# The second mixture of experts with its first product by Strassen's algorithm, in 3 passes of 768 tokens

## The chip, the cores and the metric

The kernel runs on one core of one Trainium2 chip. The metric is device time in microseconds (us) of one execution, as the median of several runs. The core has five engines that take their instructions in order and wait for each other by semaphores: TensorE (PE in the profile, with its weight loads as PEld), VectorE (DVE), ScalarE (ACT), GpSimd (POOL) and SyncE (SP), which issues nearly all DMAs here.

## The reference

Three parts follow each other on 2304 tokens of 512 features: a linear attention, a first mixture of experts with one expert per token, and the part that is changed, a second mixture in which every token goes through all 8 experts.

```
def _moe2_ref(x, w_gate, w1, w2):          # x 2304 x 512, 8 experts, hidden size 1024
    logits = x @ w_gate
    P = np.exp(logits - logits.max())
    for _ in range(8):                     # Sinkhorn steps
        P /= P.sum(1, keepdims=True) + 1e-09
        P /= P.sum(0, keepdims=True) + 1e-09
        P *= N / E
    for e in range(E):
        h = np.maximum(x @ w1[e], 0.0)     # first product
        out += P[:, e:e + 1] * (h @ w2[e]) # second product
```

All tensors are float32.

## The kernel before

Precision. TensorE multiplies in a one-pass float32 type (F32R in the code). To keep float32 accuracy each operand is split in two such parts, a high part (a copy by ScalarE into F32R) and a low part (the difference, by VectorE or GpSimd), and each product is three products: high by high, high by low, low by high. So the names come in pairs: `w1h`, `w1l`, `x2h`, `x2l`, `hh`, `hl`, `w2h`, `w2l`.

The second mixture is `moe2`. It is a generator: its first part, up to `yield`, is written after the attention and prepares the weights `w1` of expert 0 while the first mixture (`moe1`) runs; the rest starts when the rows of `x2d`, the result of the first mixture in device memory, are complete. All 18 tiles of 128 tokens are loaded into `acc`, transposed on TensorE (L836) and split into `x2h` and `x2l`, which stay in SBUF for all experts. The tokens form 5 chunks, one of 256 tokens and four of 512.

For each expert, chunk and block `f` of 128 hidden features, `first` (L895) makes 12 matmuls into one PSUM tile `ph` (4 blocks of the 512 features, 3 products each), ScalarE takes the relu into `hh` (L898) and VectorE the low part `hl` (L899). `second` (L908) multiplies the block of the step before with `w2`, 3 matmuls of 512 columns for each tile of tokens, into up to 4 PSUM tiles `py` that gather over the 8 blocks; VectorE adds each finished `py`, times its gate, to `acc` (L918). So on TensorE a first product and a second product of the block before always alternate, and the relu of one block has the time of the other product to be done in.

The weights of the next expert are loaded and split (`load_w`, L784 to L791) while the last chunk of an expert runs, through three buffers `rw` of 256 KB. Router logits come from 8 matmuls per chunk during expert 0 (L847), the Sinkhorn steps (L872 to L886) follow in the last chunk of expert 0; a step has a chain of small VectorE operations with one small matmul `pc` (L881) in it.

Each engine's order is the one that a scheduler gives to the instructions as they are written. Pools give out SBUF and PSUM tiles under a tag with a number of buffers, and an instruction that writes a reused buffer waits for the last reader of its former content.

Of the kernel before, what the change touches and what calls it, by code (L numbers as in the profile page):

```python
# [7 lines left out]
F32 = mybir.dt.float32  # L8
# [10 lines left out]
P = 128  # L19
# [13 lines left out]
CHUNKS = ((0, 2), (2, 4), (6, 4), (10, 4), (14, 4))  # first tile of P tokens, tiles  # L33
NCH = len(CHUNKS)
CH = 4 * P
NH = 3
# [6 lines left out]
def attention(tc, nc, cp, q, k, v, w_phi, w_gate, w_skip, lgs, routed, stepped, keys_done, last_steps):  # L43
    """routed(bp, x, hp, lg): rows of x for one head pair are complete; lg after the last one.
    stepped(): after each step. keys_done(): after each step once the keys' tiles are released.
    last_steps(psum): before the last products"""
    with ExitStack() as ctx:
# [15 lines left out]
        # per head: [I | w_gate | w_skip], so that one product yields num, den and logits  # L63
# [88 lines left out]
        def prep_v(u):  # L152
            # v = vh + vl, with a column of ones for the denominator
# [124 lines left out]
        # work that keeps the tensor engine busy beside the steps: (unit offset, call) by step  # L278
# [39 lines left out]
        # step t: projections of t, exponentials of t - 1, transposes and products of t - 2  # L318
# [58 lines left out]
def constants(tc, nc, keep, pool):  # L377
# [4 lines left out]
    # strictly upper ones (prefix over partitions) and ones, exact in bfloat16  # L382
# [21 lines left out]
    # of each expert: the slots of more than half a slot's tokens, then (as if of 8 more) the others  # L404
# [4 lines left out]
    # tri[v, w] = 1 for w <= v  # L409
# [13 lines left out]
class Router:  # L423
    """gates and expert of each token; lists of tokens by expert; the table of slots"""
# [8 lines left out]
    def route(self, bp, lg):  # L433
# [6 lines left out]
        # gate = 1 / (sum exp(l - max) + 1e-9) for tokens that compute  # L440
# [9 lines left out]
        # first index of the maximum  # L450
# [9 lines left out]
        # rank of a token among those of its expert, and the counts  # L460
# [26 lines left out]
        # the places of two tokens differ, so the scatters need no order among themselves  # L487
# [18 lines left out]
    def scatter(self, n=NJ):  # L506
        """n more of the scatters of the batches routed last"""
        for _ in range(min(n, len(self.todo))):
            self.todo.pop(0)()

    def early_slots(self):
        """slots 0 and 1: each the next tokens of the expert with the most left of batches 0 and 1"""
# [4 lines left out]
        for i in range(2):  # L517
# [24 lines left out]
            # tokens that the early slots take, by expert  # L542
# [9 lines left out]
    def slots(self):  # L552
        """of the slots after those: numbers of full and of all, each one's expert and first place"""
# [16 lines left out]
        # first place of slot s: bs[v(s)] + SLOT * s  # L570
# [28 lines left out]
def moe1(tc, nc, c, rt, w1, w2, idx, xd, xd0, x2d, route):  # L599
    """generator: slot 0's loads; then slot 0 and the others"""  # L600
# [171 lines left out]
def moe2(tc, nc, c, w_gate, w1, w2, x2d, out):  # L772
    """generator: the first weights; then the rest"""
    with ExitStack() as ctx:
        sm = ctx.enter_context(tc.tile_pool(name="m2s", bufs=2, reuse_waits="tile"))
        wp = ctx.enter_context(tc.tile_pool(name="m2w", bufs=1, reuse_waits="tile"))
        NKB, NFB = D // P, FF // P
        w1h, w1l = [wp.tile([P, NKB, FF], F32R, name=nm) for nm in ("w1h", "w1l")]

        def load_w(src, e, i):  # L780
            r = sm.tile([P, 512], F32, name="rw", tag="rw", bufs=3)
            if src is w1:
                kb, h = divmod(i, 2)
                nc.sync.dma_start(r, w1[e, kb * P : kb * P + P, 512 * h : 512 * h + 512])  # L784
                sl = slice(512 * h, 512 * h + 512)
                dh, dl = w1h[:, kb, sl], w1l[:, kb, sl]
            else:
                nc.sync.dma_start(r, w2[e, i * P : i * P + P])
                dh, dl = w2h[:, i], w2l[:, i]
            nc.scalar.activation(dh, r, AF.Copy)  # L790
            (nc.gpsimd if i % 3 == 1 else nc.vector).tensor_tensor(dl, r, f32(dh), ALU.subtract)  # L791

        for i in range(8):
            load_w(w1, 0, i)
# [248 lines left out]
```

## Time and profile before

| what | value |
|---|---|
| median of 3 runs | 2152.64 us (2148.99 to 2154.48) |
| the profiled execution, first to last instruction | 2155.2 us |
| TensorE busy | 2078.2 us, 96% |
| VectorE, ScalarE, GpSimd busy | 793.3, 592.0, 314.5 us |
| first matmul of a first product of the second mixture | at 548.48 us |
| groups on L895 and L908 (the second mixture's two products) | 3840 and 3456 matmuls |
| share of the last chain on TensorE | 81%, of it L895 36%, L908 36% |

A row of the timeline gives start, duration, engine, line, operation, tiles and the number of instructions merged. Matmuls are pipelined, so their durations overlap: the pace is read from start to start. A row of groups gives the count, then busy time and the mean of one in ns, then the idle time of the engine ahead of them. The granted clock is a share of 2.4 GHz.

### The profile page before, as it was taken

The page shows a single profiled execution, that of the slowest core. Times are in us where ns is not written, and L with a number is a line of the kernel's source. Part 1 is how long each engine was busy: PE and PEld are TensorE (multiplying, and loading weights), DVE is VectorE, ACT ScalarE, POOL GpSimd, SP SyncE. Part 2 cuts the span into 40 slices and gives each one's busy share as a digit, 9 for nine tenths or more (in the row PEclk, how much of TensorE's full clock was granted, in tenths as well). Part 3 has the DMA queues.
Part 4 walks back from the last instruction along what each step waited for, and adds up shares of the span by engine and source line. Part 5 has one row for each costly group of instructions (what it writes and reads, how often), then busy time and mean ns, then how long its engine had stood idle before and what let it go on. Part 6 is the DMA issues. An engine that isn't in the chain of part 4 may idle for free.

```text
span 2155.2 us, 26804 instructions
## 1 busy us (share of the span) xinstructions
PE 2078.2 (96%) x10809; PEld 1772.0 (82%) x10809; DVE 793.3 (37%) x1376; ACT 592.0 (27%) x1147; POOL 314.5 (15%) x248
## 2 busy tenths in 40 slices
PE   6999878998899999999999999999999999999999
PEld 6998867887788878888888888888888888888887
DVE  6888875786311341132123212211321232122112
ACT  4776554454321241121112112211211121122110
POOL 4445244565000000000001000000100010000000
PEclk9999898999899999999999999999999999999999
DMA  4587397564300110010002001100200020011001
GB/s 92 86 124 90 54 211 173 209 229 156 128 1 1 40 40 1 1 59 20 1 1 79 1 0 35 45 0 1 64 15 1 1 78 1 1 40 35 20 20 39
DMA packets 129992, 117.93 MB, mean 55 GB/s; under 512 B 70914, under 2 KB 94210, under 8 KB 129472
## 3 DMA queue, kind: packets, MB, share of 16 engines
q1 hardware_dynamic: 126400, 109.02, 20.4%
q0 software_dynamic: 3456, 7.09, 0.9%
q8 instruction: 87, 1.43, 0.3%
q14 instruction: 49, 0.40, 0.1%
HBM read 97.64 MB, written 20.81 MB: 55 GB/s over the span
## 4 chain that ended last, share of the span: by engine, by line
PE 81%; DMA 4%; DVE 2%; issue 1%; ACT 0%; POOL 0%; POOLq 0%; SPq 0%; DVEq 0%; ACTq 0%
PE ph L895 36%; PE py L908 36%; PE ph L687 3%; PE py L721 2%; DMA xg<-xd,ix 2%; DMA rw<-in_moe_w_dram 1%; DMA xd<-x 1%; PE pn L237 1%; DVE w2l L652 0%; PE pt L836 0%; PE pg L847 0%; PE ptq L221 0%; PE pt L664 0%; DMA x2d<-yo,ix 0%; POOL w1l L652 0%
## 5 line engine op out<-in xcount | busy, mean ns | idle before, releaser
L899 DVE SCALAR_TENSOR_TENSOR hl<-ph,hh 128x512 fp32r<-128x512 f32 (+1 forms) x320 | 203.8, 637 | 1088.2 <-ACT hh L898 1088.2
L898 ACT ACTIVATE hh<-ph 128x512 fp32r<-128x512 f32 (+1 forms) x320 | 177.5, 555 | 1164.1 <-PE ph L895 1162.3
L908 PE MATMUL py<-w2h,hh 128*128 128x512 f32 x1152 | 449.9, 391 | 0.0
L908 PE MATMUL py<-w2h,hl 128*128 128x512 f32 x1152 | 449.2, 390 | 0.0
L908 PE MATMUL py<-w2l,hh 128*128 128x512 f32 x1152 | 448.7, 390 | 0.0
L895 PE MATMUL ph<-x2h,w1h 128*128 128x512 f32 (+1 forms) x1280 | 317.6, 369 | 0.7 <-ACT x2h L838 0.7
L895 PE MATMUL ph<-x2h,w1l 128*128 128x512 f32 (+1 forms) x1280 | 316.7, 369 | 0.0
L895 PE MATMUL ph<-x2l,w1h 128*128 128x512 f32 (+1 forms) x1280 | 316.0, 369 | 0.0
L895 PEld LDWEIGHTS ph<-x2h,w1h 128*128 128x128 f32 x1280 | 231.7, 189 | 45.8 <-ACT x2h L838 1.1
L895 PEld LDWEIGHTS ph<-x2l,w1h 128*128 128x128 f32 x1280 | 228.4, 189 | 39.9
L895 PEld LDWEIGHTS ph<-x2h,w1l 128*128 128x128 f32 x1280 | 228.1, 189 | 39.7
L908 PEld LDWEIGHTS py<-w2l,hh 128*128 128x128 f32 x1152 | 216.3, 188 | 45.4
L908 PEld LDWEIGHTS py<-w2h,hh 128*128 128x128 f32 x1152 | 216.5, 188 | 42.9
L908 PEld LDWEIGHTS py<-w2h,hl 128*128 128x128 f32 x1152 | 216.5, 188 | 42.4
L791 POOL TENSOR_TENSOR w2l<-rw,w2h 128x512 fp32r<-128x512 f32 x24 | 31.0, 1290 | 1262.6 <-ACT w2h L790 1262.6
L358 POOL TENSOR_TENSOR fl<-f,fh 128x1024 fp32r<-128x1024 f32 (+1 forms) x40 | 86.5, 2162 | 117.8 <-DVE fh L357 64.5
L918 DVE SCALAR_TENSOR_TENSOR acc<-py,lg,acc 128x512 f32<-128x512 f32 x126 | 85.9, 741 | 2.1 <-PE py L908 2.1
L790 ACT ACTIVATE w2h<-rw 128x512 fp32r<-128x512 f32 x64 | 40.2, 633 | 82.0 <-PE py L908 74.7
L652 DVE TENSOR_TENSOR w2l<-r,w2h 128x512 fp32r<-128x512 f32 x48 | 60.5, 1260 | 3.5
L790 ACT ACTIVATE w1h<-rw 128x512 fp32r<-128x512 f32 x64 | 39.0, 630 | 73.8 <-DMA rw<-in_moe_w_dram 63.7
L687 PE MATMUL ph<-xTh,w1h 128*128 128x256 f32 x288 | 48.5, 292 | 11.1 <-ACT xTh L666 7.0
L791 DVE TENSOR_TENSOR w1l<-rw,w1h 128x512 fp32r<-128x512 f32 x40 | 33.5, 849 | 68.5 <-ACT w1h L790 47.5
(228 smaller groups left out, 2308.2 us busy)
## 6 DMA issues: line engine op xcount, KB each, us to landing
r<-in_moe_w_dram SPq DMA_DIRECT2D x76, 512.0 KB, 5.8
rw<-in_moe_w_dram SPq DMA_DIRECT2D x128, 256.0 KB, 2.8
xd<-x SPq DMA_DIRECT2D x12, 576.0 KB, 15.4
qt<-in_q_dram SPq DMA_DIRECT2D x32, 144.0 KB, 3.6
x2d<-x SPq DMA_DIRECT2D x8, 576.0 KB, 3.8
out_dram<-acc SPq DMA_DIRECT2D x18, 256.0 KB, 2.1
kt<-in_k_dram SPq DMA_DIRECT2D x32, 128.0 KB, 2.7
vt<-in_v_dram SPq DMA_DIRECT2D x32, 128.0 KB, 3.0
```

Of the source, the lines that this page charges most:

```text
L237: nc.tensor.matmul(pn, w[:, b, h, fb], r[:, h, fb, b], start=(c == 0), stop=(c == 5))
L358: nc.gpsimd.tensor_tensor(fl[:, :n], f[:, :n], f32(fh)[:, :n], ALU.subtract)
L652: (nc.gpsimd if pool and i % 3 == 1 else nc.vector).tensor_tensor(dl, src, f32(dh), ALU.subtract)
L687: nc.tensor.matmul(ph, wt[:, kb, f * P : f * P + P], xt[:, kb], start=(n == 0), stop=(n == 11))
L721: nc.tensor.matmul(py, ht[:, f, a * P : a * P + P], wt[:, f], start=(n == 0), stop=(n == 23))
L790: nc.scalar.activation(dh, r, AF.Copy)
L791: (nc.gpsimd if i % 3 == 1 else nc.vector).tensor_tensor(dl, r, f32(dh), ALU.subtract)
L895: nc.tensor.matmul(ph, wt[:, kb, f * P : f * P + P], xt[:, kb], start=(m == 0), stop=(m == 11))
L898: nc.scalar.activation(hh, ph, AF.Relu)
L899: nc.vector.scalar_tensor_tensor(hl, ph, 0.0, f32(hh), ALU.max, ALU.subtract)
L908: nc.tensor.matmul(ys[i], ht[:, i * P : i * P + P], wt[:, f], start=(f == 0 and n == 0), stop=(f == NFB - 1 and n == 2),)
L918: nc.vector.scalar_tensor_tensor(acc[:, t], ys[i], lg[:, t, e : e + 1], acc[:, t], ALU.mult, ALU.add)
```

## The change

`moe2` is written anew; attention, first mixture and router are as before, but for removed comments and constants.

The tokens go in 3 passes of 768, each made of a half of 384 tokens from either half of the batch. Within a pass all experts run, each in 2 "quads" of 4 blocks of 128 hidden features, so there are 48 quads. A quad's first product is a 2 x 2 block product: features in 2 halves, hidden blocks in 2 x 2, tokens in 2 halves. Strassen's algorithm, in Winograd's form with shared sums, gives the four results from 7 block products of half the depth instead of 8, at the price of sums of blocks ahead of the products (of weights on GpSimd, `sums_w1`, of tokens on VectorE, `sums_x`) and of sums of products behind them (`s`, `v`, `z`, `c22`, `c21`, on ScalarE and VectorE). Each of the 7 sums of weights and of tokens is split in high and low part.

A quad has 2 groups `g` of 7 products. Between them stand the second products of the quad before, as `piece`s of 12 matmuls for one tile of tokens; a piece is added to `acc` for each quad, so twice for each expert. In a group the PE order is: product 1 into `a`, product 6 into `b`, product 2 on top of `a` (after ScalarE has copied `a` to `s`), product 7 into `d`, a piece, product 5 on top of `b` (after VectorE has added `s` to `b` and ScalarE copied it to `v`), a piece, product 3 on top of `b`, product 4 on top of `d`, a piece.

Weights `w1` of a quad come as two DMAs of 512 KB into `r1`, which has one buffer; `w2` through two buffers `r2`. The token tiles are loaded and transposed one by one for each pass; 12 of the 18 a second time, ahead of the Sinkhorn steps, for their logits alone (`other_logits`).

```
+        def load_w1(n):
...
+            r = wp.tile([P, NKB, 2, QF], F32, name="r1", tag="r1")
+            for h in range(2):
+                nc.sync.dma_start(
+                    r[:, :, h],
+                    w1[e, :, 512 * h + QF * q : 512 * h + QF * q + QF].rearrange("(b p) f -> p b f", p=P),
+                )
...
+        def sums_w1(n):
...
+            a11, a12, a21, a22 = r[:, 0:2, 0], r[:, 2:4, 0], r[:, 0:2, 1], r[:, 2:4, 1]
...
+            g = nc.gpsimd
+            g.tensor_tensor(s1, a21, a22, ALU.add)
+            g.tensor_tensor(s2, s1, a11, ALU.subtract)
+            g.tensor_tensor(a21, a11, a21, ALU.subtract)
+            wsrc[n] = {1: a11, 6: s2, 2: a12, 7: a21, 5: s1, 3: a12, 4: a22}
+
+        def split_w1(n, k):
...
+            i = ORDER[k]
+            src = wsrc[n]
+            if i == 3:
+                nc.gpsimd.tensor_tensor(src[3], src[2], src[6], ALU.subtract)
+            h, l = [wp.tile([P, 2, QF], F32R, name=nm, tag=nm, bufs=9) for nm in ("wch", "wcl")]
+            nc.scalar.activation(h, src[i], AF.Copy)
+            nc.vector.tensor_tensor(l, src[i], f32(h), ALU.subtract)
...
+        def mm(dst, n, g, i, start, stop):
...
+            for w, x in ((wh, xh), (wh, xl), (wl, xh)):
+                for kb in range(2):
+                    nc.tensor.matmul(
+                        dst, w[:, kb, sl], x[:, kb], start=(start and m == 0), stop=(stop and m == 5),
+                        skip_group_check=True,
+                    )
...
+        def group(n, g, fill):
...
+            def after(k):
+                if last and k + 2 < 7:
+                    split_w1(n + 1, k + 2)
+                if new_pass:
+                    split_x(k)
...
+            mm(a, n, g, 1, True, False)
+            after(0)
+            s = copied(a, "s")
+            mm(b, n, g, 6, True, False)
+            after(1)
+            nc.vector.tensor_tensor(b, b, s, ALU.add)
+            v = copied(b, "v")
+            mm(a, n, g, 2, False, True)
+            after(2)
+            relu(n, g, 0, 0, a, nc.vector)
+            mm(d, n, g, 7, True, False)
+            after(3)
+            fill[0]()
+            mm(b, n, g, 5, False, False)
+            after(4)
+            z = copied(b, "z")
+            fill[1]()
+            mm(b, n, g, 3, False, True)
+            after(5)
+            relu(n, g, 1, 0, b, nc.vector)
+            c22 = big.tile([P, TW], F32, name="c22", tag="c22")
+            nc.vector.tensor_tensor(c22, d, z, ALU.add)
+            mm(d, n, g, 4, False, True)
+            after(6)
+            relu(n, g, 1, 1, c22, nc.vector)
+            c21 = big.tile([P, TW], F32, name="c21", tag="c21")
+            nc.vector.tensor_tensor(c21, d, v, ALU.add)
+            relu(n, g, 0, 1, c21, nc.vector)
+            fill[2]()
...
+                if g == 0:
+                    load_w1(n + 1)
+                    load_w2(n, 0)
+                    load_w2(n, 1)
...
+                    sums_w1(n + 1)
+                    split_w1(n + 1, 0)
+                    split_w1(n + 1, 1)
+                group(n, g, fill)
+                if g:
+                    load_w2(n, 2)
+                    load_w2(n, 3)
...
-        def first(e, ch, f):
...
-            for wt, xt in ((w1h, xh), (w1h, xl), (w1l, xh)):
-                for kb in range(NKB):
-                    nc.tensor.matmul(ph, wt[:, kb, f * P : f * P + P], xt[:, kb], start=(m == 0), stop=(m == 11))
...
```

A piece is the second product as before (12 matmuls of 512 columns for a tile of tokens and 4 blocks), into `py`, which has 2 buffers. `TW` is 384, `QF` 256, `ORDER` is (1, 6, 2, 7, 5, 3, 4); `wch` and `wcl` have 9 buffers, so the split of product k of the next quad (k from 2) waits for the buffer that the product k - 2 of this quad's second group releases.

How the change moves instructions, on TensorE. Before, in the middle of an expert (`ph` is a first product, `py` a second):

```order
L895 MATMUL ph<-x2h_9136,w1l 128x512 x4
L908 MATMUL py<-w2h,hh 128x512
L908 MATMUL py<-w2h,hl 128x512
L908 MATMUL py<-w2l,hh 128x512
L908 MATMUL py<-w2h,hh 128x512
```

Now, at the start of a quad (`xch`, `xcl` are the split sums of tokens, `wch`, `wcl` those of weights; the first row is the end of a piece):

```order
L988 MATMUL py<-w2l,hh_12621 128x512
L954 MATMUL pa<-xch,wch 128x384 x2
L954 MATMUL pa<-xcl,wch 128x384 x2
L954 MATMUL pa<-xch,wcl 128x384 x2
L954 MATMUL pb<-xch,wch 128x384 x2
L954 MATMUL pb<-xcl,wch 128x384 x2
L954 MATMUL pb<-xch,wcl 128x384 x2
L954 MATMUL pa<-xch,wch 128x384 x2
L954 MATMUL pa<-xcl,wch 128x384 x2
L954 MATMUL pa<-xch,wcl 128x384 x2
L954 MATMUL pd<-xch,wch 128x384 x2
L988 MATMUL py<-w2h,hh_12698 128x512
```

Between the first and the second use of `pa` one other product stands, where before a whole second product stood between a `ph` and what its relu is needed for.

On ScalarE. Before, around the change from one expert to the next (`rw` are raw weights):

```order
L790 ACTIVATE w2h<-rw 128x512
L898 ACTIVATE hh<-ph 128x512
L790 ACTIVATE w2h<-rw 128x512
L790 ACTIVATE w1h<-rw 128x512 x2
L898 ACTIVATE hh<-ph 128x512
```

Now, around the start of a quad (`r_12946` is the buffer of raw `w1` of the quad after it, `s_13076` the sum s2 of those weights, `r_12934` and `r_12940` raw `w2`, `s<-pa` the copy that product 2 waits for):

```order
L970 ACTIVATE hh_12910<-c_12902 128x384
L820 ACTIVATE wch<-r_12946 128x512
L943 ACTIVATE w2h<-r_12934 128x512
L970 ACTIVATE hh_12916<-c_12914 128x384
L943 ACTIVATE w2h<-r_12940 128x512
L820 ACTIVATE wch<-s_13076 128x512
L962 ACTIVATE s<-pa 128x384
L943 ACTIVATE w2h<-r_12949 128x512
L962 ACTIVATE v<-pb 128x384
L943 ACTIVATE w2h<-r_12955 128x512
L970 ACTIVATE hh_12987<-pa 128x384
```

The split of the next quad's s2 now stands ahead of the copy `s` of this quad.

On GpSimd. Before, in the second mixture (low parts of the next expert's weights):

```order
L791 TENSOR_TENSOR w2l<-rw,w2h 128x512 x2
L791 TENSOR_TENSOR w1l<-rw,w1h 128x512
L791 TENSOR_TENSOR w2l<-rw,w2h 128x512
L791 TENSOR_TENSOR w1l<-rw,w1h 128x512 x2
L791 TENSOR_TENSOR w2l<-rw,w2h 128x512
```

Now, for one quad (the sums of the raw weights `r_12946`, with two low parts of `w2`):

```order
L807 TENSOR_TENSOR s_13075<-r_12946 128x512
L808 TENSOR_TENSOR s_13076<-s_13075,r_12946 128x512
L809 TENSOR_TENSOR r_12946<-r_12946 128x2x256
L944 TENSOR_TENSOR w2l<-r_12940,w2h 128x512
L944 TENSOR_TENSOR w2l<-r_12955,w2h 128x512
L818 TENSOR_TENSOR r_12946<-r_12946,s_13076 128x2x256
```

Before, GpSimd had only low parts of weights; now its first two rows of a quad make what ScalarE's split of s2 reads.

## Rows read from the trace of the kernel before

**Rows 1.** The page, first line.
```profile
span 2155.2 us, 26804 instructions
```

**Rows 2.** Stretches: length, busy by engine (instructions), PEclk, DMA share, GB/s.
```profile
700.00:800.00 100.00, 96.67 (x475) 79.75 (x475) 41.57 (x109) 36.15 (x64) 7.72 (x6) 1.00 0.15 43
1100.00:2100.00 1000.00, 1000.00 (x4636) 837.13 (x4635) 227.89 (x343) 161.87 (x283) 38.80 (x30) 1.00 0.07 23
```

**Rows 3.** The chain that ended last, its end: start, us, what.
```profile
2145.48 3.42 PE py L908 x15
```

**Rows 4.** Timeline of PE: first products of 512 and 256 columns, a Sinkhorn matmul.
```profile
1001.64 1.07 PE L895 MATMUL ph<-x2h,w1h 128*128 128x512 f32 x4
...
1004.36 0.39 PE L908 MATMUL py<-w2h,hh 128*128 128x512 f32 x1
...
769.37 0.64 PE L895 MATMUL ph<-x2h,w1h 128*128 128x256 f32 x4
...
770.80 0.40 PE L908 MATMUL py<-w2h,hh 128*128 128x512 f32 x1
...
767.46 0.36 PE L881 MATMUL pc<-cs,ones_f 128*128 128x8 f32 x2 [0.98 <-DVE cs L879]
767.68 0.48 PE L908 MATMUL py<-w2l,hh 128*128 128x512 f32 x1
```

**Rows 5.** Timeline: end of a first product on PE, its relu on ACT, then DVE.
```profile
1096.84 0.39 PE L908 MATMUL py<-w2h,hh 128*128 128x512 f32 x1
...
1097.04 0.60 ACT L898 ACTIVATE hh<-ph 128x512 fp32r<-128x512 f32 x1 [4.84 <-PE ph L895]
...
1097.67 0.69 DVE L899 SCALAR_TENSOR_TENSOR hl<-ph,hh 128x512 fp32r<-128x512 f32 x1 [4.75 <-ACT hh L898]
```

**Rows 6.** Groups by shape: count, busy us, mean ns, idle before.
```profile
L898 ACT ACTIVATE hh<-ph 128x512 fp32r<-128x512 f32 x226 | 135.2, 598 | 932.0 <-PE ph L895 931.1 <-DVE w2l L791 0.7
L790 ACT ACTIVATE w2h<-rw 128x512 fp32r<-128x512 f32 x56 | 35.5, 635 | 76.2 <-PE py L908 74.7 <-DMA rw<-in_moe_w_dram 1.1
L898 ACT ACTIVATE hh<-ph 128x256 fp32r<-128x256 f32 x56 | 21.3, 380 | 99.5 <-PE ph L895 98.7 <-DVE rs L875 0.8
...
L258 DVE TENSOR_TENSOR x<-po,rd 128x384 f32<-128x384 f32 x24 | 13.2, 549 | 0.2
...
L791 POOL TENSOR_TENSOR w2l<-rw,w2h 128x512 fp32r<-128x512 f32 x21 | 27.1, 1291 | 1239.5 <-ACT w2h L790 1239.5
```

**Rows 7.** DMA issues: engine, count, KB each, median us to landing.
```profile
rw<-in_moe_w_dram SPq DMA_DIRECT2D x128, 256.0 KB, 2.8
...
x2d<-x SPq DMA_DIRECT2D x8, 576.0 KB, 3.8
...
acc<-x2d SPq DMA_DIRECT2D x3, 1024.0 KB, 9.4
```

**Rows 8.** Timelines of DVE and POOL where both work on SBUF tiles.
```profile
762.86 0.69 DVE L791 TENSOR_TENSOR w2l<-rw,w2h 128x512 fp32r<-128x512 f32 x1
...
381.04 8.20 DVE L652 TENSOR_TENSOR w2l<-r,w2h 128x512 fp32r<-128x512 f32 x1
...
381.20 3.80 POOL L652 TENSOR_TENSOR w2l<-r,w2h 128x512 fp32r<-128x512 f32 x3
384.95 3.73 POOL L652 TENSOR_TENSOR w1l<-r,w1h 128x512 fp32r<-128x512 f32 x3
...
411.56 1.45 DVE L652 TENSOR_TENSOR w2l<-r,w2h 128x512 fp32r<-128x512 f32 x1
...
412.42 5.14 POOL L652 TENSOR_TENSOR w1l<-r,w1h 128x512 fp32r<-128x512 f32 x3
```

**Rows 9.** Transposes on PE, and the chain at the start of the second mixture.
```profile
534.52 1.03 PE L664 MATMUL pt<-ident,xg 128*128 128x128 f32 x8
...
542.83 2.89 DMA acc<-x2d
...
548.48 5.49 PE ph L895 x24
```

More of the change, by code (lines that the diff above doesn't have):

```diff
@@ new lines, in split_w1 @@
+        def split_w1(n, k):
+            if n >= len(quads):
+                return
+            i = ORDER[k]
[5 more added lines that the diff above has]
+            nc.vector.tensor_tensor(l, src[i], f32(h), ALU.subtract)
+            wc[n, i] = (h, l)
+        load_w1(0)
@@ L961, in moe2, with load_w2 @@
-        second(*prev)
+        hs = {}
+        w2s, w2r = {}, {}
+        def load_w2(n, b):
+            _, e, q = quads[n]
+            f = (b % 2) * 4 + 2 * q + b // 2
+            r = big.tile([P, D], F32, name="r2", tag="r2", bufs=2)
+            nc.sync.dma_start(r, w2[e, f * P : f * P + P])
+            h, l = [big.tile([P, D], F32R, name=nm, tag=nm, bufs=6) for nm in ("w2h", "w2l")]
+            nc.scalar.activation(h, r, AF.Copy)
+            (nc.gpsimd if b % 2 else nc.vector).tensor_tensor(l, r, f32(h), ALU.subtract)
+            w2s[n, b] = (h, l)
@@ new lines, in moe2, with piece @@
+        accs = {}
+        def piece(n, half, i):
+            if n < 0:
+                return
+            ps_, e, q = quads[n]
+            t = tiles(ps_, half)[i]
+            py = ps.tile([P, D], F32, name="py", tag="Y", bufs=2)
+            m = 0
+            for b in range(4):
+                hh, hl = hs[n, b, half]
+                wh, wl = w2s[n, b]
+                for ht, wt in ((hh, wh), (hl, wh), (hh, wl)):
+                    nc.tensor.matmul(py, ht[:, i * P : i * P + P], wt, start=(m == 0), stop=(m == 11))
+                    m += 1
+            if e == 0 and q == 0:
+                accs[t] = big.tile([P, D], F32, name="acc", tag="acc", bufs=2 * TB)
+                if ps_ == 0:
+                    nc.scalar.activation(accs[t], py, AF.Copy)
+                else:
+                    nc.scalar.activation(accs[t], py, AF.Copy, scale=lg[:, t, 0:1])
+            elif e == 0 and ps_ == 0:
+                nc.vector.tensor_tensor(accs[t], py, accs[t], ALU.add)
+                nc.scalar.activation(accs[t], accs[t], AF.Copy, scale=lg[:, t, 0:1])
+            else:
+                nc.vector.scalar_tensor_tensor(accs[t], py, lg[:, t, e : e + 1], accs[t], ALU.mult, ALU.add)
+            if e == E - 1 and q == NQ - 1:
+                nc.sync.dma_start(row(t, 1), accs[t])
@@ L964, in tile_kernel @@
+        for h in range(2):
+            for i in range(TB):
+                piece(len(quads) - 1, h, i)
 @with_exitstack
```

265 lines of the change are left out of this document (121 added, 144 removed).

## The prediction

> **What bounds the kernel now.** I read the page's first line, the stretches, the end of the chain, the timeline of TensorE, and then the groups of the engines that feed it. In the steady part of the second mixture TensorE is busy for 1000 of 1000 us at a granted clock of 1.00, the full 2.4 GHz; ScalarE is busy for 16% of it, VectorE for 23%, GpSimd for 4% [rows 2]. The last chain ends with matmuls back to back [rows 3]. So the end is set by the number and pace of matmuls. The pace, start to start: 12 matmuls of 512 columns take 2.72 us (0.227 each), 12 of 256 columns 1.43 us (0.119) [rows 4]. From the end of a first product, taken as the next matmul's start, ScalarE begins 0.20 us later and VectorE 0.03 us after ScalarE has ended [rows 5].
>
> **First products.** Before: 64 blocks, each with four chunks of 512 columns and one of 256, 64 x (4 x 2.72 + 1.43) = 787.8 us. After: 48 quads x 2 groups x 7 products x 6 matmuls = 4032 matmuls of 384 columns. No row has 384; midway between the two paces is 0.173, the ends are 0.119 and 0.227, and I take the middle since both paces are the columns at 2.4 GHz plus 0.013. That makes 697.2 us, a gain of **90.6 us**. Second products stay 3456 matmuls, 783.4 us. A group is then 7 x 1.04 + 3 x 2.72 = 15.4 us of TensorE, a quad 30.9.
>
> **Waits within a quad.** Before, a relu had a second product of 2.72 us as its cover; now product 2 needs the copy s of product 1 with only product 6 (1.04 us) between. Durations: a 384-wide ScalarE copy 0.49 us (midway between 0.598 and 0.380), a 384-wide VectorE operation 0.55, a 512-wide ScalarE split 0.63, a GpSimd operation 1.29 [rows 6], a VectorE split 0.69 [rows 8]. Count from the start of product 1.
> Second group: ScalarE's order has the split of the next quad's weights ahead of s. That split needs a buffer that product 1 releases: 1.24 + 0.63 + 0.49 + 0.05 = 2.41, against 2.08 when product 6 ends. Wait 0.33 us. The later ones have room: z is read by 9.6 (product 3 at 11.0), c22 is ready at 10.4 (product 4 at 12.0).
> First group: the split ahead of s is that of s2, a sum for the next quad. GpSimd makes it from r1, which has one buffer. The chain: the last split that reads r1 runs behind product 5 of the second group (end at 8.25): 8.45 + 0.63 + 0.03 + 0.69 = 9.8 us into it, 6.0 before the next quad. Then two DMAs of 512 KB. No row shows 1 MB alone: 256 KB lands in 2.8 us, 576 KB in 3.8, a 1 MB load behind others in 9.4 [rows 7]. I take the slope of the first two, 2.8 + 0.75 x 3.2 = 5.2, nearest to 3.8; the ends are 3.8 and 9.4. Weights are there 0.8 us before the quad, and s1 and s2 follow on GpSimd.
> There VectorE is in the way: its splits read two SBUF tiles. Alone such a split takes 0.69 us; beside GpSimd's the two alternate, 1.45 on VectorE and 1.71 each on GpSimd; and once one split stood for 8.20 us while six GpSimd operations ran through [rows 8]. In between the sum s2 and the next there is a dependence, which lets VectorE in, so I take alternation: s1 ends at 0.55, VectorE's split at 1.2, s2 at 2.45, its split on ScalarE at 3.1, s at 3.6, product 2 starts at 3.65 instead of 2.08. Wait 1.5 us (0.25 if the weights land 0.7 earlier and nothing collides).
> Behind s in ScalarE's queue stand a w2 split, v, a w2 split and the relu of a; product 5, at about 8.4, needs v, which is there by 6.8. So 1.83 us for each quad. 46 quads (the first two are counted below): **+84 us**, between 27 and 122.
> The Trainium skill, page "DMA: Bandwidth & Descriptors", section "Anatomy of one DMA — SWDGE (gpsimd) path", fits about 2.0 us plus bytes over 436 GB/s, for another way of issuing; an estimate from it is 4.4 us for 1 MB, and by that the first group's wait would be 0.9 and the whole 2142 us. No row here has a 1 MB load by itself.
>
> What else a quad has is hidden beside TensorE's 30.9 us: on VectorE 29 operations of about 0.65 us, 19 us; on ScalarE 11 splits and 14 copies or relus, 14 us; on GpSimd 6 operations, 8 us; and 2 MB of weights, now loaded in each of the three passes, 7 us of DMA by the slope above. Without that cover each would cost its own time; only the chain through s lies bare.
>
> **Start, Sinkhorn steps, passes.** Before, TensorE ends at about 2150.8 [rows 3]; from 548.5 [rows 9] these are 1602.3 us, 1571.2 of them products: 31.1 us go to transposes, logits, Sinkhorn and a slow clock at the start (24 matmuls of 256 columns took 5.49 us there instead of 2.9 [rows 9]).
> After: 18 tiles each pay 4 transposes at 0.13 (8 in 1.03 [rows 9]) and 4 logit matmuls at 0.22 (such a pair in the trace [rows 4]), 25 us. Up to the first Sinkhorn step TensorE's order holds 25 products and three pieces, 34 us; with the slow clock 4, that is 63 us from 545.9. The tiles themselves come one by one, since two buffers serve rows and transposes: a load of 2.9 [rows 9] and 0.6 for the transposes, 12 x 3.5 behind six in pairs, to 597. TensorE's sum, 609, decides: 26.5 us lost beyond products. Eight Sinkhorn steps: a small matmul cost TensorE 0.98 us of wait [rows 4]; VectorE is now half busy, so 10 us (5 to 25). Each of two passes more: 24 transposes, 3.1 us, and about 4 of waits where VectorE also splits the new tokens; 14. Sum 50.5 against 31.1, **+19 us** (5 to 50).
>
> **First mixture.** The sums for the first two quads stand on GpSimd ahead of a gather of the first mixture: **+4 us** (0 to 10). End: the last piece, its VectorE addition and the output DMA are as before.
>
> **Sum.** -90.6 + 84 + 19 + 4 = +17 on the profiled span of 2155.2 [rows 1]: 2172. The median of the runs, 2152.64, lies 2.6 below that span, so **2169 us**.
>
> **Rivals.**
> (1) The weights come in time: r1 lands and is summed without a collision, waits 0.25 + 0.33 for each quad, 46 x 0.58 = 27 instead of 84: 2112 us, faster. For it: GpSimd ran only 31 operations in 1000 us with no wait of TensorE [rows 2]. Against: the 8.20 us row, and 1 MB would have to land within 4.5 us. It decides as soon as the first group's wait is below 1 us.
> (2) VectorE is starved: s1, s2 and two more GpSimd operations run through, as in the 8.20 us row. Then the w2 split is late by 4 us, the buffer r2 is refilled late, ScalarE's w2 split ahead of v waits for it, and product 5 waits 1.35 more, with s 0.6 earlier: 46 x 0.8 = 38 more, 2207 us. Against: s2 must wait for s1.
> The Trainium skill, "SBUF — State Buffer", section "SBUF: two separate sides", says the pair of ports shared by VectorE and GpSimd is an exclusive lock held for a whole instruction, the other fully blocked. The 1.45 and 8.20 us rows agree; it leaves open who is next, which is what parts (2) from the forecast.
> (3) The start costs more: TensorE, in order, stands at each of the 12 extra loads, 12 x 2.5 = 30 more: 2199 us. Scheduling puts products between them, which speaks against it.
> (4) The clock falls: after waits of 1.5 us in 32 the chip grants the lower level, 1.2 GHz, as it did behind the idle time ahead of the second mixture (5.49 us for 2.9 [rows 9]). One twentieth of 1480 us at half speed is 74 more: 2243 us. Against: 700 to 800 us had 3.3 us of idle TensorE at 1.00 [rows 2].
> That the saving is not there at all I rule out: the products are counted.
>
> **Chances.** Forecast 0.55 (its own range 2140 to 2195), (1) 0.21, (2) 0.12, (3) 0.08, (4) 0.04. About 0.3% is what a measurement of this kernel tells from no change: under 2146 lie (1) and 0.05 of the forecast, 0.26; 2146 to 2159 has 0.12; above 0.62. Leaving out half of (1)'s lower side and (4), 8 in 10 lie between 2108 and 2222.
>
> **What would show it.** In the steady part, matmuls of 384 columns 0.173 apart, no slower clock; TensorE idle ahead of product 2 by 0.3 us in one group and about 1.5 in the next, released by ScalarE's s, and ScalarE idle before the split of s2, released by GpSimd; GpSimd's first sum released by the DMA of r1, landing some 5 us after its issue; VectorE splits of 1.4 to 2 us there. Wrong it is if product 2 does not wait, if another product waits more (5 for v, 4 for c22), or if the start loses over 40 us.

## The result, and the profile after

The changed kernel takes **2176.55 us** (median of 5, 2166.98 to 2179.45) against 2148.99 (median of 5, 2147.27 to 2154.48) of the kernel before, 1.0115 times as long, interval 1.009 to 1.014. The forecast was 2169, within 2108 to 2222, and slower at 0.62. The sign and the place of the wait were right. That the total came out near was in part luck: three terms were mis-sized by 16 to 25 us each, and the errors cancelled for the most part.

The profiled execution after has a span of 2165.3 us (its own time 2166.98, the shortest of the five). Its stretches, with the columns of [rows 2]:

```profile
535.00:600.00 65.00, 62.28 (x321) 54.79 (x322) 28.52 (x53) 30.60 (x61) 9.19 (x7) 0.77 0.34 105
600.00:700.00 100.00, 93.31 (x478) 81.03 (x477) 70.94 (x153) 42.12 (x83) 21.71 (x15) 1.00 0.20 64
700.00:1040.00 340.00, 331.05 (x1640) 295.57 (x1639) 214.81 (x305) 132.19 (x262) 93.01 (x64) 1.00 0.21 66
1040.00:1130.00 90.00, 83.06 (x404) 73.65 (x403) 58.05 (x84) 40.71 (x83) 20.11 (x14) 0.94 0.28 91
1130.00:1500.00 370.00, 358.91 (x1778) 320.49 (x1777) 228.87 (x323) 146.30 (x289) 103.02 (x71) 1.00 0.21 67
```

Against [rows 2], TensorE no longer works without a gap in the steady part: 97% (331.05 of 340), at a clock of 1.00. VectorE has gone from 23% to 63%, ScalarE from 16% to 39%, GpSimd from 4% to 27%. What TensorE waits for from 700 us on (total, times, longest):

```profile
PE pa L954 <- ACT s L962: 40.4, 43, 2.3
PE pt L854 <- DMA xr<-x2d: 7.2, 3, 3.5
```

That is the forecast's wait for `s`, with 4.9 us more of it ahead of 700. One quad of the timeline shows its chain, first group, quad start at 1325.35:

```profile
1319.01 0.93 SPq L793 DMA_DIRECT2D r<-in_moe_w_dram  x2
1324.11 1.40 POOL L807 TENSOR_TENSOR s<-r 128x512 f32<-128x512 f32 x1 [10.71 <-DMA r<-in_moe_w_dram]
1324.27 1.78 DVE L944 TENSOR_TENSOR w2l<-r,w2h 128x512 fp32r<-128x512 f32 x1
1325.35 0.51 PE L954 MATMUL pa<-xch,wch 128*128 128x384 f32 x2
1325.59 1.61 POOL L808 TENSOR_TENSOR s<-s,r 128x512 f32<-128x512 f32 x1
1325.98 1.64 DVE L971 SCALAR_TENSOR_TENSOR hl<-c,hh 128x384 fp32r<-128x384 f32 x1
1327.23 0.63 ACT L820 ACTIVATE wch<-s 128x512 fp32r<-128x512 f32 x1 [2.40 <-POOL s L808]
1327.77 0.47 ACT L962 ACTIVATE s<-pa 128x384 f32<-128x384 f32 x1
1328.30 0.61 PE L954 MATMUL pa<-xch,wch 128*128 128x384 f32 x2 [0.69 <-ACT s L962]
```

Read it from the load down. Two DMAs are issued at 1319.01 and land 5.1 us later (I had taken 5.2). Then s1 and s2 follow on GpSimd, alternating with VectorE operations that take 1.64 and 1.78 us beside them instead of 0.55 and 0.69. ScalarE stands 2.40 us before the split of s2, and only behind that comes `s`. Product 2 starts at 1328.30, where 1327.45 would have been next. A quad takes 32.20 us without any longer wait (starts at 1293.15, 1325.35, 1357.55); the kernel before needed 32.73 for as much (its 1571.2 us of products over 48). When the load lands later, the wait is longer, as in the quad that started at 1162.73 (2.5 us):

```profile
1156.41 0.93 SPq L793 DMA_DIRECT2D r<-in_moe_w_dram  x2
1162.95 1.29 POOL L807 TENSOR_TENSOR s<-r 128x512 f32<-128x512 f32 x1 [12.16 <-DMA r<-in_moe_w_dram]
1164.32 1.28 POOL L808 TENSOR_TENSOR s<-s,r 128x512 f32<-128x512 f32 x1
1165.63 0.63 ACT L820 ACTIVATE wch<-s 128x512 fp32r<-128x512 f32 x1 [3.42 <-POOL s L808]
1166.74 0.48 ACT L962 ACTIVATE s<-pa 128x384 f32<-128x384 f32 x1
```

The load was issued as far ahead of its quad as the other (6.3 us) and took 6.5 us. The sums take 1.29 and 1.28 us, the time that [rows 6] has for an operation of GpSimd, so this longer wait has no collision in it.

The second group, where I had forecast 0.33 us, does not wait: product 1 starts at 1309.71, product 2 at 1311.81, 2.1 us later, back to back.

```profile
1309.71 0.51 PE L954 MATMUL pa<-xch,wch 128*128 128x384 f32 x2
1310.61 0.63 ACT L820 ACTIVATE wch<-r 128x512 fp32r<-128x512 f32 x1 [1.94 <-PE pa L954]
1311.15 0.47 ACT L962 ACTIVATE s<-pa 128x384 f32<-128x384 f32 x1
1311.81 0.52 PE L954 MATMUL pa<-xch,wch 128*128 128x384 f32 x2
```

The split ahead of `s` begins 0.90 us after the start of product 1, not 1.24: it overwrites a high part, and the last two of a product's six matmuls read the low part only.

The pace of the matmuls, from rows of 1302 to 1307 us:

```profile
1302.10 0.40 PE L988 MATMUL py<-w2h,hh 128*128 128x512 f32 x1
1304.85 0.51 PE L954 MATMUL pb<-xch,wch 128*128 128x384 f32 x2
1305.90 0.51 PE L954 MATMUL pd<-xch,wch 128*128 128x384 f32 x2
```

A second product (12 matmuls) takes 2.75 us where [rows 4] had 2.72, and a first product (6) takes 1.05, that is 0.175 for a matmul instead of 0.173.

### The profile page after: what moved, and what is told of

Read it like the earlier page. It is cut to its first block, busy times and chain, and to the rows that moved or that the text cites. A ratio compares the mean times of both kernels' runs of the same rounds, so it can differ in the third digit from the quotient of the medians.

```text
span 2165.3 us, 30290 instructions
## 1 busy us (share of the span) xinstructions
PE 2036.6 (94%) x11135; PEld 1824.4 (84%) x11135; DVE 1424.8 (66%) x2244; ACT 955.2 (44%) x1933; POOL 673.5 (31%) x486
## 4 chain that ended last, share of the span: by engine, by line
PE 68%; DMA 8%; POOL 5%; DVE 3%; ACT 2%; issue 2%; SPq 0%; POOLq 0%; DVEq 0%; ACTq 0%
PE py L988 33%; PE pb L954 11%; PE pd L954 9%; PE pa L954 8%; DMA x2d<-yo,ix 3%; DMA r<-in_moe_w_dram 3%; POOL s L808 3%; PE ph L683 2%; PE py L717 2%; PE pl L861 1%; ACT s L962 1%; POOL s L807 1%; PE pt L854 1%; DVE wcl L821 1%; DMA xd<-x 1%
## 5 line engine op out<-in xcount | busy, mean ns | idle before, releaser
L1000 DVE SCALAR_TENSOR_TENSOR acc<-py,lg,acc 128x512 f32<-128x512 f32 x264 | 197.6, 748 | 210.7 <-PE py L988 208.8
L988 PEld LDWEIGHTS py<-w2l,hh 128*128 128x128 f32 x1152 | 216.4, 188 | 48.1
L820 ACT ACTIVATE wch<-r 128x512 fp32r<-128x512 f32 x240 | 151.3, 631 | 235.0 <-PE pb L954 125.8
L821 DVE TENSOR_TENSOR wcl<-r,wch 128x512 fp32r<-128x512 f32 x240 | 198.9, 829 | 75.2 <-ACT wch L820 74.5
L944 POOL TENSOR_TENSOR w2l<-r,w2h 128x512 fp32r<-128x512 f32 x96 | 144.2, 1502 | 232.9 <-ACT w2h L943 207.4
L943 ACT ACTIVATE w2h<-r 128x512 fp32r<-128x512 f32 x192 | 120.3, 628 | 144.3 <-DMA r<-in_moe_w_dram 140.5
L971 DVE SCALAR_TENSOR_TENSOR hl<-c,hh 128x384 fp32r<-128x384 f32 x192 | 148.2, 772 | 31.5 <-ACT hh L970 31.5
L954 PE MATMUL pb<-xch,wch 128*128 128x384 f32 x576 | 148.9, 339 | 0.0
L954 PE MATMUL pb<-xcl,wch 128*128 128x384 f32 x576 | 148.0, 338 | 0.0
L954 PE MATMUL pa<-xch,wch 128*128 128x384 f32 x384 | 105.1, 354 | 45.3 <-ACT s L962 45.3
L954 PE MATMUL pb<-xch,wcl 128*128 128x384 f32 x576 | 147.6, 337 | 0.0
```

The source lines that it names most:

```text
L820: nc.scalar.activation(h, src[i], AF.Copy)
L821: nc.vector.tensor_tensor(l, src[i], f32(h), ALU.subtract)
L943: nc.scalar.activation(h, r, AF.Copy)
L944: (nc.gpsimd if b % 2 else nc.vector).tensor_tensor(l, r, f32(h), ALU.subtract)
L954: nc.tensor.matmul(dst, w[:, kb, sl], x[:, kb], start=(start and m == 0), stop=(stop and m == 5), skip_group_check=True,)
L971: eng.scalar_tensor_tensor(hl, src, 0.0, f32(hh), ALU.max, ALU.subtract)
```

## The experiments

Each is an edit of the changed kernel unless said otherwise. The ratios are to the kernel before in the same set.

**The same programs again** (two runs: before, and after).

> The kernel before, unchanged, for a second profile. In the two profiles at hand the second mixture's first transposes start at 545.9 us (before) and 534.9 (changed kernel), although the code ahead of them is nearly the same; I had expected +4 there. Theory A (the granted clock in the first 300 us differs from execution to execution, 0.93 against 0.97 in the first 100 us): this profile's start of the second mixture may lie anywhere between 535 and 550. Theory B (the change really shortens the first mixture, since its ScalarE and GpSimd orders shifted): 546 within 2 us again. The second mixture itself takes 1604.7 us from there to the start of the last matmul, within 2 us, by both.

> The changed kernel, unchanged, for a second profile and times beside the others of this set. Theory A (clock differs by execution early on): the first transposes anywhere between 535 and 550, the second mixture 1626 us from there, within 6, so that the time is 2167 to 2180. Theory B (the change shortens the first mixture): 535 within 2 us, time 2167 to 2170. Ratio to before 1.009 to 1.014 by A.

Before: 2154.25 us, the second mixture's first transposes at 543.8, 1604.1 us from there to the start of the last matmul (1604.7 in the first profile). After: 2177.17, ratio 1.0118 (1.0085 to 1.015), first transposes at 535.5, 1635.9 us from there (1626.2 in the first). The early start came again, which speaks for theory B; but the run below without the pass changes has the very order of after up to there, and started at 544.4. The two runs that only move splits of later quads started at 549.8 and 545.5. So the start of the second mixture differs by 10 us and more between executions, and the two profiles do not size my +4 for the first mixture.

The two profiles of after differ by 9.7 us in the second mixture. The waits for `s` are 2.7 us of that (45.3 and 48.1 us, longest 3.0). Most of the rest is the clock: in the second profile it fell behind long waits for `s` also where the first has 1.00. Here is one stretch of 10 us of each, both behind a wait of 2.2 to 2.3 us (first the first profile):

```profile
1165.00:1175.00 10.00, 7.73 (x38) 6.93 (x39) 4.55 (x6) 4.10 (x8) 4.82 (x4) 1.00 0.23 71
1170.00:1180.00 10.00, 7.75 (x32) 6.93 (x31) 3.32 (x4) 3.61 (x7) 6.00 (x5) 0.83 0.22 72
```

The first quad took 33.79 us, the second 35.30. From 700 us on the two profiles have seven waits for `s` of over 2.2 us, and behind five of them TensorE ran for a while at its lower level, 0.50.

**The split of s2 behind s.**

```
-nc.scalar.activation(h, src[i], AF.Copy)
+ins = nc.scalar.activation(h, src[i], AF.Copy)
+if i == 6 and n >= 2:
+    tc.add_manual_dep(
+        ins.ins,
+        s_copy[n - 1].ins.name,
...
```

> Only ScalarE's order changes: the split of s2 (the next quad's second sum) stands behind the copy s of the first group instead of ahead of it. My theory (product 2 of the first group waits, 0.93 us at least and 1.14 in the mean, because that split holds s back until GpSimd has made s2 from the late load): the wait goes, a steady quad takes 31.2 to 31.3 us instead of 32.2, 46 x 1.14 = 52 us less, about 2124 us, faster than before by 1%. Rival 1 (the late sum only moves its wait: the two w2 splits and v now stand behind the split of s2, and product 5 or the next second products wait for them): no gain to half of it, 2150 to 2176. Rival 2 (the 0.93 us is the hand-over from TensorE to ScalarE and back, not the split): no change.

2227.79 us, ratio 1.0354 (1.0319 to 1.0389): much slower. Product 2 never waits any more, and product 5 waits 74.4 us in 39 places for `v`. Rival 1 had named this kind of wait, but not that the kernel would become slower than after:

```profile
1333.34 0.49 ACT L969 ACTIVATE s<-pa 128x384 f32<-128x384 f32 x1 [1.82 <-PE pa L961]
1333.92 0.63 ACT L820 ACTIVATE wch<-s 128x512 fp32r<-128x512 f32 x1
1335.25 0.63 ACT L950 ACTIVATE w2h<-r 128x512 fp32r<-128x512 f32 x1 [0.70 <-DMA r<-in_moe_w_dram]
1339.84 0.63 ACT L950 ACTIVATE w2h<-r 128x512 fp32r<-128x512 f32 x1 [3.96 <-DMA r<-in_moe_w_dram]
1340.38 0.47 ACT L969 ACTIVATE v<-pb 128x384 f32<-128x384 f32 x1
1340.90 0.62 PE L961 MATMUL pb<-xch,wch 128*128 128x384 f32 x2 [1.78 <-ACT v L969]
```

The scheduler had answered the one edge by putting both `w2` splits ahead of `v` (in the changed kernel one stood ahead and one behind), and the second of them waits 3.96 us for its load. So an order can be worse than the wait that it removes; what the split of s2 costs was still open.

**The split of s2 behind v**, with the second `w2` split held behind `v` too (the same kind of edge).

> Only ScalarE's order: the split of s2 stands behind v and the two w2 splits, instead of ahead of s; the order of the w2 splits about v is as in the changed kernel (one ahead, one behind). In the run with the split right behind s, both w2 splits had also come ahead of v, and product 5 waited up to 3.3 us for v, which stood behind a w2 split that waited 3.96 us for its load. My theory (the s2 split ahead of s is the whole of the first group's wait, and the loss of that run came from the second w2 split ahead of v): no wait of product 2, none of product 5, a quad of 31.2 to 31.3 us, about 2120 us. Rival (the w2 loads are late whatever the order, since GpSimd's sums hold the low part that frees their buffer, so a wait stays somewhere): 32 us and more for a quad, 2160 or above.

2134.31 us, ratio 0.9926 (0.9898 to 0.9955). Most quads take 31.21 us, and no wait for `s` or `v` is left from 700 us on. One instruction's place was worth 0.99 us in each quad, and some 43 us in all, a little less than expected, since a few quads still wait for `z` or c22 (3.5 us together).

**Two buffers for the weights' tile r1.**

```
-r = wp.tile([P, NKB, 2, QF], F32, name="r1", tag="r1")
+r = (pools[0] if n % 2 == 0 else pools[-1]).tile([P, NKB, 2, QF], F32, name="r1", tag="r1")
...
-t3, t2 = [big.tile([P, 2, TW], F32, name=nm, tag=nm) for nm in ("t3", "t2")]
+t3, t2 = b12, b22
```

> The weights' tile r1 gets a second buffer, so that its load starts a quad earlier; to make room the sums of the tokens are written over one another, so the products are of wrong tokens, with the same operations and sizes. ScalarE's order keeps the split of s2 ahead of s. My theory (the chain starts at the late load): s2 is there long before the quad, the wait of product 2 goes, 31.2 to 31.4 us for a steady quad, about 2124 us. Rival 1 (the sums on GpSimd collide with VectorE wherever they stand, and the wait is that collision): 32.0 to 32.5 for a quad, 2165 to 2180. Rival 2 (hand-over): no change, as above.

2115.94 us, ratio 0.984 (0.9809 to 0.9872); a quad takes 31.21 to 31.24 us. The split of s2 still stands ahead of `s`, so it is the late load that makes it late: with the load a quad earlier, the same sums on GpSimd beside the same VectorE hold nothing up. They collide as before: the second sum takes 1.63 us in the mean, 1.57 in after. Both ends of the chain are thus shown, the order and the load. The collision alone (rival 1) makes no wait, and the hand-over (rival 2) none either.

**The same with room made properly**: the second r1 as above, t3 written over b11 and c22 over `z`, once those are read.

> The second buffer for r1 again, now with room made by writing two sums over tiles that are no longer read (t3 over b11, c22 over z), so that the whole computation is done. Expected from the run before with two buffers (31.22 us for a quad, no wait in the steady part, ratio 0.984): 2110 to 2122 us, the fastest so far. Rival (z is now held until the relu of c22 has read it, and product 5 of the next group waits to copy into it): 31.5 to 32.5 for a quad.

2118.30 us, ratio 0.9855 (0.983 to 0.988), 31.21 to 31.24 us for a quad; c22 in `z` is waited for 4.1 us at the two pass changes and not at all elsewhere.

**The sums on VectorE**, ScalarE's order held as it was.

```
-g = nc.gpsimd
+g = nc.vector
```

> The three sums of the weights go from GpSimd to VectorE, with ScalarE's order as in the changed kernel (the split of s2 ahead of s). Theory A (the load's landing starts the chain, and in VectorE's queue the first sum is followed by an accumulation that must await the last second product of the quad): s1 is summed in 0.7, s2 only after the accumulation, 1.5 us into the quad, so product 2 still waits, 0.5 to 0.9 us for a quad; but with no GpSimd operation beside, the long waits of up to 2.4 us go: 2150 to 2172 us. Theory B (the collision of VectorE and GpSimd on their ports makes the wait): the wait goes, 31.3 us for a quad, 2120 to 2135.

2153.20 us, ratio 1.0003 (0.9991 to 1.0016), as theory A had it. Product 2 still waits 0.8 us in nearly every quad, now evenly (32.30 to 32.34 us for a quad); one wait of 2.4 is left, and the quad behind a pass change has none:

```profile
1348.98 1.78 DVE L807 TENSOR_TENSOR s<-r 128x512 f32<-128x512 f32 x1
1350.68 0.74 DVE L1007 SCALAR_TENSOR_TENSOR acc<-py,lg,acc 128x512 f32<-128x512 f32 x1
1351.34 0.68 DVE L808 TENSOR_TENSOR s<-s,r 128x512 f32<-128x512 f32 x1
1352.05 0.63 ACT L820 ACTIVATE wch<-s 128x512 fp32r<-128x512 f32 x1 [3.57 <-DVE s L808]
1353.11 0.62 PE L961 MATMUL pa<-xch,wch 128*128 128x384 f32 x2 [0.82 <-ACT s L969]
```

One GpSimd split is still beside the first sum (1.78 instead of 0.68). The pass changes became shorter than expected of it: 2.7 and 3.6 us over a steady quad in the first quad of a change, 1.1 under it in the second, where after had 8.1 and 8.9, then 3.2 and 1.7 over it.

**No change of tokens between passes** (all passes work on the first pass's tokens).

```
-new_pass = last and e == E - 1 and q == NQ - 1 and ps_ + 1 < NPASS
+new_pass = False
```

The calls of `load_x` and `sums_x` for the later passes are left out too.

> Leaves out the change of tokens between passes: all three passes use the first pass's tokens (no load, no transposes, no sums or splits for the second and third). The changed kernel's profile has 8.1 + 3.2 + 0.8 us beyond a steady quad at the first change and 8.9 + 1.7 + 1.3 at the second, 24 together, where I had predicted 14. Theory: those 24 us go, and nothing else: periods of 32.2 there, about 2177 - 24 = 2153. Rival (part of it is the accumulators' change, with its output DMAs and the new weights of expert 0, or the clock's fall for another cause): 5 to 12 us remain, 2158 to 2165.

2157.09 us, ratio 1.0032 (1.0014 to 1.0049): 20 us less than after in the same kind of set (2177.17), and the quads at the changes take 32.17 to 32.23. The time lies between those of the theory and the rival; by the quads nothing of the price stays. The two changes cost 20 to 24 us; I had predicted 14.

**No logits for the 12 later tiles.**

```
-fill = [lambda i=i: [other_logits(t) for t in others[4 * i : 4 * i + 4]] for i in range(3)]
+fill = [lambda i=i: None for i in range(3)]
```

> Leaves out the logits of the 12 tiles of later passes (their loads, transposes and matmuls), so the Sinkhorn steps run on zeros there. From the first transposes to the fifth quad the changed kernel took 163.4 us, 51 more than its steady quads would; I had predicted 36.5 more. By the trace, the 12 tiles' own matmuls are 12 x (4 x 0.11 + 8 x 0.11) = 16 us at full clock. Theory A (the start is dear for these matmuls and their loads): 51 falls to 30 to 36, about 2160 us. Theory B (the start is dear because the clock stands at its lower level for some 30 us whatever runs there, and by Sinkhorn's steps): it falls by 8 to 14 only, 2164 to 2170.

2165.46 us, ratio 1.0077 (1.0046 to 1.0107), 12 less than after. From the first transposes to the fifth quad 150.1 us, 37.6 more than steady quads, where after had 51: theory B. Most of the start's price is not the extra logits.

**Work for TensorE ahead of the second mixture**, on the two-buffer version.

```
...
+for i in range(78):
+    nc.tensor.matmul(warm[:, 0:QF], wh[:, i % 2, 0:P], wl[:, i % 2], start=(i == 0), stop=(i == 77))
 load_x(0, True)
```

> The two-buffer version with 78 matmuls of 256 columns, whose result nobody reads, ahead of the second mixture's first transposes, in the 9.4 us in which TensorE waits for the first tokens' load; the scheduler, which counts them, then also moves some extra logits behind later products. Theory A (the clock stands at its lower level for 30 us from there because TensorE had been idle for 9.4 us): it stays at 1.00, and the start gains 8 to 14 us, 2104 to 2111 against 2118 for the version without. Theory B (the low level comes of the sparse transposes and logits themselves, 8.6 us of 10 busy at half clock being 40% at full): the clock falls a little later all the same, gain 0 to 5.

2123.97 us, ratio 0.9871 (0.9855 to 0.9888): no gain on 2118.30. The matmuls could not begin before 534.44 us (they waited 4.91 us for a branch of the first mixture) and put the transposes off to 545.74. The stretches from there, and then the first 27 us of the two-buffer version without these matmuls (transposes from 535.07):

```profile
539.00:548.90 9.90, 8.03 (x68) 7.79 (x67) 3.57 (x3) 2.96 (x6) 4.74 (x4) 1.00 0.52 167
540.00:550.00 10.00, 8.12 (x65) 7.89 (x64) 3.77 (x4) 2.96 (x6) 5.84 (x4) 0.95 0.48 160
550.00:560.00 10.00, 6.32 (x29) 5.41 (x27) 1.89 (x4) 3.40 (x8) 1.32 (x2) 0.50 0.48 157
560.00:570.00 10.00, 9.06 (x39) 7.93 (x38) 2.08 (x4) 3.30 (x9) 1.27 (x1) 0.50 0.34 105
570.00:580.00 10.00, 9.27 (x45) 8.51 (x44) 8.62 (x13) 5.76 (x9) 0.00 (x0) 0.69 0.10 29
...
535.00:562.00 27.00, 23.84 (x100) 21.24 (x100) 9.71 (x17) 12.35 (x26) 5.02 (x4) 0.50 0.45 138
```

Under the added matmuls the clock rose to 1.00 (539 to 548.9). Then TensorE did four transposes, waited 1.88 us and did the first logits, and the clock was at 0.50, the lower level of 1.2 GHz, for 27 us (549 to 576). Without the added matmuls it was there for 27 us too. So 9.4 us of idle time ahead of the transposes are not needed for the fall, as theory B has it. From the first transposes to the start of the last matmul both versions take the same, 1573.1 and 1573.0 us: the added matmuls gave nothing back, and the two profiles differ by the later start (545.7 against 535.1). They did not fill the idle time as planned, since the branch held them; what a clock at 1.00 throughout the start would be worth stays untested.

**The pace by itself.**

> The pace by itself: nothing but matmuls with weights changed for each, in stretches of 360 of 384 columns, 360 of 512, 360 of 256, 360 of 384, a mix in the kernel's turns (3 and 1 first products about each second product), and 360 of 320 columns; no other engine works beside them, and nothing of the reference is computed. Theory A (the 0.1755 us for 384 columns, where 0.173 was expected, and the 0.2297 in second products, 0.2267 before, are TensorE's own): 0.1755 here too, and in the mix the same first nine slow matmuls of each second product (0.224 to 0.241). Theory B (they come of other engines' traffic beside it): 0.173 to 0.174 and 0.2267 in every stretch, the mix too.

Matmuls of one width alone keep the pace that I had taken: 0.1733 us for 384 columns, 0.2267 for 512, 0.120 for 256 (0.147 for 320). In the mix, nothing but TensorE working:

```profile
210.15 1.20 PE L38 MATMUL pb<-xt,wt 128*128 128x384 f32 x6
211.19 1.20 PE L38 MATMUL pa<-xt,wt 128*128 128x384 f32 x6
...
262.15 2.92 PE L46 MATMUL pa<-vt,ht 128*128 128x512 f32 x12
264.91 1.23 PE L38 MATMUL pa<-xt,wt 128*128 128x384 f32 x6
265.98 2.92 PE L46 MATMUL pa<-vt,ht 128*128 128x512 f32 x12
```

Six in a row of one width: 1.04 us. Behind a change of width the 12 of 512 columns take 2.76 instead of 2.72, and the six of 384 take 1.07. The first nine of each 12 are irregular (229, 233, 236, 224, 231, 236, 228, 233, 230 ns, then 227), in the kernel much as here. For the second products it is TensorE's own, as theory A says; theory B's 0.173 holds among matmuls of one width. The trace of the kernel before had it already: six matmuls of 512 columns behind 256-wide ones take 1.39 us, six behind their own width 1.36.

```profile
979.45 0.40 PE L908 MATMUL py<-w2h,hh 128*128 128x512 f32 x1
...
980.84 0.64 PE L895 MATMUL ph<-x2h,w1h 128*128 128x256 f32 x4
```

For the first products the run agrees with the kernel in the mean only. Three of a group's seven stand behind a change of width, and 3 x 1.07 and 4 x 1.04 give 1.05 for one. But in the kernel one that follows another of its own width takes 1.05 as well, where it takes 1.04 here; what slows those stays open. Not each change costs, either: behind 512 columns, six matmuls of 256 take 0.71 us (0.72 among themselves) and six of 320 take 0.875 (0.88), each seen once. Why a change from 512 to 384 or from a smaller width to 512 does cost stays open.

**Two buffers and the sums on VectorE.**

> Both edits that helped: the second buffer for r1 (whole computation) and the three sums on VectorE. In the two-buffer version a pass change still took 8.1 us beyond a steady quad (7.6 and 0.5 over its two quads, with VectorE at 10 of 10 us in one stretch); with the sums on VectorE and one buffer it took 2.7 in the first of its two quads and 1.1 less than a steady one in the second, since a sum on VectorE takes 0.68 us where GpSimd's takes 1.4 to 1.6 and blocks VectorE meanwhile. Theory A (GpSimd's sums make the pass changes dear): steady quads stay at 31.2, a change costs 2 to 4, 2106 to 2112 us. Theory B (VectorE's queue becomes late in the steady part instead, 3 more operations for each quad): 31.5 or more for a quad, 2125 and above.

**2105.93 us**, ratio 0.9772 (0.9744 to 0.98), the fastest. Waits of TensorE from 700 us on, and two stretches:

```profile
PE pt L855 <- DMA xr<-x2d: 2.7, 6, 0.8
```

```profile
1100.00:1500.00 400.00, 400.00 (x1998) 360.81 (x1997) 260.78 (x404) 163.60 (x324) 55.26 (x38) 1.00 0.23 71
1700.00:2050.00 350.00, 350.00 (x1750) 316.06 (x1749) 230.96 (x358) 139.94 (x279) 48.30 (x33) 1.00 0.21 64
```

TensorE works 750 of 750 us again. A quad takes 31.21 to 31.24 us, a pass change 4.6 and 4.3 instead of 8.1 (7.6 and 0.5) in the version with GpSimd's sums, less than theory A's gain but on its side. The second mixture takes 1557.9 us from its first transposes, 46.5 less than before: this much of the saving of a product in eight is to be had.

## Why the prediction was right or wrong

From the first transposes to the start of the last matmul the profiled executions took 1604.7 us before and 1626.2 after. By the prediction's steps:

| step | predicted | measured |
|---|---|---|
| first products | -90.6 | -82.2 (4032 x 0.175 = 705.6) |
| second products | 0 | +10 (48 x 6 x 0.035) |
| waits in the quads | +84 | +59 (45.3 us of idle time in 45 waits, and 45 x 0.30) |
| start, Sinkhorn steps, passes | +19 | +35 (1626.2 less 705.6, 793.5 and 59 is 68; before 1604.7 less 1571.2 is 33.5) |
| sum | +12 | +21.5 |

The 0.30 is what a wait costs beyond the idle time that the profile shows: the 37 quads from 698 us on that are not at a pass change have 32.1 us of idle time and are 43.2 us longer than 37 quads without a wait (31.22 us).

**Products, their saving too large by 18 us** (8 in the first, 10 in the second). The midway 0.173 was right for matmuls of one width (0.1733). What I did not have is that the kernel changes width six times in a group, and that TensorE alone loses time in such a mix, in products of both kinds. Before, widths mixed in one chunk of five only, and the pace in [rows 4] is that of the others and of the 256-wide matmuls in a row; the loss of 512-wide ones behind 256-wide ones stood in that trace, and I had not used it.

**Waits, mis-sized by 25 us.** The mechanism of the first group stands row by row: release, load of 5.1 us, sums on GpSimd alternating with VectorE, split of s2, `s`, product 2. The size was 0.98 us in most quads (32.20 against 31.22) and up to 3.3 in others, in the mean 1.3, not 1.5. In most quads the last reader of r1 was done 0.6 us earlier than I had counted, so that s1 began 1.24 us ahead of the quad instead of 0.8, and the two sums took 3.1 us instead of 3.25. The longer part of the error, 15 us, is the second group's 0.33: I took the buffer as released by the whole product, when four of its six matmuls release the high part, and that wait is not there at all.

The Trainium skill, page "DMA: Bandwidth & Descriptors", section "Anatomy of one DMA — SWDGE (gpsimd) path", fits DMAs that GpSimd issues; from it came the estimate of 4.4 us for the load and with it a wait of 0.9. This load, issued by SyncE, took 5.1 and in the longer case 6.5, so the measurement decides against the figure here. That the usual wait came out near 0.9 does not speak for it: an earlier release and shorter sums made that.

**Rival (2), VectorE starved** (38 us more; 46 x 0.8 is 37), did not come in the kernel as it is. Its place, product 5 waiting for `v` behind a late `w2` split, is just what the first reordering produced, without starving: a second `w2` split ahead of `v` was enough.

**Start and passes, too small by 16 us.** The start lost 51 us beyond steady quads, and over 40 was one of the prediction's own signs of being wrong: on this term it was. In the start the clock was at 0.50 for 30 us of transposes, logits and few products, where I had allowed 4 us for a slow clock; by an estimate that is up to 11 more (half of 30 us, less the 4), which no run shows by itself. The two pass changes cost 20 to 24 instead of 14: a wait of 3.5 us for the first new tokens, a stretch at the lower clock (0.94 in the mean of 1040 to 1130), and a first group whose `s` comes 1.6 us later than usual. Rival (3)'s mechanism, a wait at each of 12 loads, was not there: from 545 to 700 us no wait for a tile of tokens appears.

**First mixture, +4**: cannot be told from the 10 us by which executions differ in it.

**Rival (1)** (2112) is what the kernel becomes when the load has its second buffer: 2118. Its condition, weights in time, was the right one to name; that its number is near is chance, since it still holds 27 us of waits and no such wait is left there. I had let it decide by a first group's wait below 1 us. That was a poor sign: in most quads the idle time is 0.69, and yet the chain and the collision are those of the forecast. (Its row has 30 operations of GpSimd, not 31.)

**Rival (4)** did not come as a whole: the steady clock is 1.00, and the usual wait leaves it there. But its mechanism is seen behind five of the seven waits of over 2.2 us in the two profiles, at some 1.5 us for a quad (35.30 against 33.79).

The forecast of 2169 was made from an execution of 2155.2; four of the five runs of after lie 7 to 12 us above its profiled one. Their mean clock was 0.971 to 0.976 against 0.978; where they lost it no profile of them shows, but the second profile of after (2175.6, 0.973) lost its 10 us mostly to longer waits for `s` and to the lower clock behind them.

## What to carry to other kernels

A saving on the bound engine is kept only where each product's short chain (here copy, add, copy) has its whole path on time: look in every in-order queue for the instruction ahead of the short one, and follow it back to its load. Here a single split, 0.63 us long and not needed for another 31 us (product 6 of the next quad), took 43 us of the saving, and either its place or one more buffer of its source gave it back. When an order is repaired by an edge, read the new order of all the engine's neighbours: the scheduler's answer to one edge cost 50 us more.

## What the hardware showed that I had not expected

- Some changes of the matmul's width cost TensorE: 12 of 512 columns take 2.76 us behind 384-wide ones and 2.72 among themselves, 6 of 384 take 1.07 behind 512-wide ones and 1.04, with no other engine at work; 6 of 256 behind 512-wide ones lost nothing (0.71 against 0.72).
- The lower clock came under transposes and logits right behind 78 matmuls under which it had risen to 1.00, not only behind 9.4 us of idle time; and in the steady part it came behind five of seven waits of 2.2 to 2.5 us.
- A VectorE operation on SBUF tiles with two inputs is held by GpSimd's in both forms seen here: a scalar_tensor_tensor of 0.55 us took 1.64, a subtraction of 0.69 took 1.78.
